# Where six subtractions run and in which order two loads are issued, in an attention and expert kernel on one core

## The chip, the cores and the metric

The kernel runs on one core of a Trainium2 chip. The metric is the device time of one execution in microseconds; the time before is the median of 3 runs, 727.25 us (727.22 to 727.77). The engines are named as in the profile: PE is TensorE's matmuls, PEld its weight loads, DVE is VectorE, ACT is ScalarE, POOL is GpSimd, and SP is the sync engine, whose list issues most of the DMAs. Each engine works through its own list of instructions in order.

## The reference, cut to what matters

```python
def _attn_ref(u, v, z):                       # u, v: 4 x 3072 x 256, z: 4 x 3072 x 64
    scores = (1.0 / S) * np.matmul(z, z.transpose(0, 2, 1))
    out = np.matmul(np.maximum(scores, 0.0) ** 2, v)
    return u * out
...
x = attn_out.reshape(B * S, D)
x = _moe_ref(x, w_gate, w1, w2, capacity)     # 8 experts, top 1, capacity slots each
return _moe2_ref(x, w_in, w_out)              # x * sigmoid-gated MLP
```

The gate sends each token to one of 8 experts, and an expert keeps only its first 384 tokens. Most rows beyond the first 3,500 tokens or so are dropped, so that the kernel works out attention for the first batch (3072 queries) and for one chunk of 384 queries of the second batch, and goes on only if some expert is not full by then.

## The kernel before, in words

All matrix products are done in a split form: a number is written as a head in fp32r and a low part, the rest in fp32r, and a product is the sum of two or three matmuls on heads and low parts. The splits are elementwise work for ACT, DVE and POOL.

**Attention.** The queries go in chunks: six of 512 queries (batch 0), then one of 384 queries (batch 1). A chunk takes KT = 24 steps, one per tile of 128 keys, so the stretch has 168 ticks. `attend` (L514) writes out the order by hand. In tick t it puts into the lists: `scores(t)` (L339: two matmuls, a relu on ACT L347, a square on DVE L352, or on ACT L350 in each fourth tick), `square(t-1)` (L355: the head ah by an ACT cast L360, the low part al by a DVE subtraction L361), `values(t-3)` (L364: six matmuls, the last two of which take al), and then whatever was booked for tick t with `at(t, f)`, in the order of booking (`Stream`, L250). "al(k)" below is the subtraction of step k; it stands in tick k+1, and TensorE takes it in tick k+3.

**Keys and values.** The keys of a batch are held in six tiles kz (groups g = 0 to 5 of four key tiles) and the values in six pairs of tiles big. For z, the raw tile zr (two buffers, shared with the raw queries zq of a chunk) is loaded by SP (`load_z`, L281). Rows 0 to 63 and 64 to 127 both hold the same z. `split_z` (L294) writes the head into all 128 partitions of kz (L161 on POOL) and then replaces partitions 64 to 127 by the low part (L297, 64x512, two operands in SBUF). For v, `load_v` (L286) loads one of two raw tiles rawt, and `split_v` (L299) makes the heads with two ACT casts (L163) and the low parts with two POOL subtractions (L303), each 128x512.

**The second batch.** While the last full chunk (ticks 120 to 143) still runs, the tiles kz and big are refilled for batch 1 group by group (L849 to L853). Group g is split in tick 127, 132, 135, 139, 143, 147 for g = 0 to 5, and its loads are booked four ticks earlier (for g = 1, five ticks). Its keys are needed from tick 144 + 4g on.

**What else stands in POOL's list there.** The result of a chunk is gated, transposed, given its expert and scattered to disp with four indirect DMAs that POOL issues (`route` L495, `scatter` L463); for the fifth chunk they stand in tick 131, just ahead of the split of group 1, and what they send is finished by DVE (slots L457 to L461, row numbers L446). The raw queries of the last chunk are split on POOL in tick 138 (L161, L337). The weights w_in and w_out arrive as 64-bit words and are converted in the ticks between (`Convert`, L172): ACT L202, L203, DVE L205, L208, L210, L213, an ACT cast, and POOL L217, L220, L222.

**After attention** come the experts (about 319 to 466 us) and the gated MLP (to the end), with TensorE as good as without gaps.

Of the kernel before, what the change touches and what calls it, by code (L numbers as in the profile page):

```python
# [28 lines left out]
def attention_moe_swish_kernel(  # L29
# [13 lines left out]
    nc = tc.nc  # L43
# [206 lines left out]
    class Stream:  # L250
# [5 lines left out]
        def at(self, t, f):  # L256
            self.todo.setdefault(t, []).append(f)
# [541 lines left out]
    def batch(b):  # L799
        return Batch(lambda r, n: v[b, r:r + n, :], lambda c, n: zT[:, b * S + c:b * S + c + n])  # L800


    b0, b1 = batch(0), batch(1)
# [4 lines left out]
    at = st.at  # L808
# [39 lines left out]
            at(c * KT - 6, lambda c=c: chunks[c].split(nc.gpsimd))  # L848
    for g in range(NG):  # L849
        t = TL - KT + (g + 1) * GK + LAG  # L850
        at(t - 4, lambda g=g: (b1.load_z(g), b1.load_v(g)))
        t += g == 1
        at(t, lambda g=g: (b1.split_z(g, nc.gpsimd, nc.gpsimd), b1.split_v(g, eng=nc.scalar)))  # L853

    free = [t for t in range(CV_A, TL + CV_B) if (t < KT or CV_OFF <= (t - LAG + 1) % KT < KT - 1)]
    cvs = list(conversions())
# [402 lines left out]
```

## Time and profile before

| | |
|---|---|
| median of 3 runs | 727.25 us (727.22 to 727.77) |
| the profiled execution's own time | 727.94 us |
| its span, from the first to the last instruction | 726.2 us |
| mean granted TensorE clock | 0.999 |
| busy: PE, PEld | 712.7 us, 634.3 us |
| busy: DVE, ACT, POOL | 521.0 us, 502.6 us, 264.7 us |

The span is 1.74 us shorter than the execution's own time, and the profiled execution is 0.69 us above the median. In the timeline each row is a start, a duration, the engine, the line of the kernel, the operation, its output and inputs, and in square brackets how long the engine sat idle just before and what ended that. A row with x2 merges two instructions that follow each other.

### The profile page before, as it was taken

Reading aid. Unit: us, or ns where it says so; the run is one execution under the profiler, and the core shown is the slowest. Engines: PE = TensorE matmul, PEld = TensorE weight load, DVE = VectorE, ACT = ScalarE, POOL = GpSimd, SP = SyncE. Lnnn points to the kernel's source line nnn. Section 1 sums busy time; section 2 is a strip of 40 time slices with the busy share of each in tenths; the row PEclk is TensorE's granted clock in tenths of the full one; section 3 lists DMA queues with packets and bytes.
Section 4 is the critical chain, followed back from the end, with each engine's and each line's share of the span. In section 5 each row is a group of like instructions: output and inputs, shape, how many; then the busy total and the mean of one; then the engine's idle time right before and its main releaser. Section 6 shows DMA issues by size and latency. Waiting matters only on the chain.

```text
span 726.2 us, 11358 instructions
## 1 busy us (share of the span) xinstructions
PE 712.7 (98%) x3954; PEld 634.3 (87%) x3955; DVE 521.0 (72%) x955; ACT 502.6 (69%) x986; POOL 264.7 (36%) x246
## 2 busy tenths in 40 slices
PE   9999999999999998999999999999999999999995
PEld 6888888888888887998999999999999999989895
DVE  6786877877778774863677777779767966676780
ACT  6777778777787896865676666667657755665771
POOL 8770505405243289455577676000004000040004
PEclk9999999999999999999999999999999999999999
DMA  5843515234056323363555554101001000010001
GB/s 181 288 146 123 183 35 188 70 116 146 10 199 212 98 93 98 112 190 107 192 195 178 172 177 140 58 27 54 1 1 59 1 1 1 1 58 1 1 1 59
DMA packets 50668, 72.18 MB, mean 99 GB/s; under 512 B 3446, under 2 KB 38684, under 8 KB 50608
## 3 DMA queue, kind: packets, MB, share of 16 engines
q1 hardware_dynamic: 48160, 65.03, 27.4%
q0 software_dynamic: 2448, 6.39, 2.4%
q8 instruction: 32, 0.52, 0.3%
q14 instruction: 28, 0.23, 0.1%
HBM read 46.05 MB, written 25.77 MB: 99 GB/s over the span
## 4 chain that ended last, share of the span: by engine, by line
PE 51%; issue 1%; POOL 0%; POOLq 0%; ACT 0%
PE ps_s L782 18%; PE ps_s L242 8%; PE ps_a L242 8%; PE ps_a L1071 6%; PE ps_a L1072 5%; PE ps_a L1073 5%; PE ps_a L600 1%; POOL out L793 0%; POOLq L1255 0%; ACT qt L606 0%; POOLq L793 0%
## 5 line engine op out<-in xcount | busy, mean ns | idle before, releaser
L242 PE MATMUL ps_a<-ah,big 128*128 128x512 f32 (+1 forms) x672 | 183.1, 389 | 2.7 <-ACT ah L360 2.5
L242 PEld LDWEIGHTS ps_a<-ah,big 128*128 128x128 f32 x672 | 123.9, 188 | 24.1 <-ACT ah L360 3.1
L361 DVE TENSOR_TENSOR al<-ps_s,ah 128x512 fp32r<-128x512 f32 (+1 forms) x168 | 111.3, 663 | 29.3 <-ACT ah L360 29.3
L347 ACT ACTIVATE r<-ps_s 128x512 f32<-128x512 f32 (+1 forms) x168 | 98.3, 585 | 42.0 <-PE ps_s L242 34.9
L352 DVE TENSOR_TENSOR ps_s<-ps_s,r 128x512 f32<-128x512 f32 (+1 forms) x132 | 89.2, 676 | 41.6 <-ACT r L347 40.1
L793 POOL DMA_INDIRECT out<-rows,ids x24 | 25.0, 1044 | 242.8 <-ACT rows L790 235.0
L782 PEld LDWEIGHTS ps_s<-wo,big 128*128 128x128 f32 x792 | 103.2, 190 | 6.1 <-ACT rows L790 1.1
L242 PE MATMUL ps_s<-qt,kz 128*128 128x512 f32 (+1 forms) x336 | 106.1, 392 | 0.5 <-POOL qt L337 0.5
L782 PE MATMUL ps_s<-wo,big 128*128 128x256 f32 x792 | 105.2, 282 | 0.8 <-ACT rows L790 0.8
L568 POOL TENSOR_TENSOR big<-rawt,big 128x512 fp32r<-128x512 f32 x64 | 89.7, 1429 | 42.4 <-ACT big L163 37.8
L242 PE MATMUL ps_a<-al,big 128*128 128x512 f32 (+1 forms) x336 | 101.1, 382 | 0.0
L360 ACT CAST ah<-ps_s 128x512 fp32r<-128x512 f32 (+1 forms) x168 | 95.6, 569 | 3.9 <-DVE ps_s L352 3.6
L242 PEld LDWEIGHTS ps_s<-qt,kz 128*128 128x128 f32 x336 | 63.6, 191 | 12.0 <-POOL qt L337 0.9
L242 PEld LDWEIGHTS ps_a<-al,big 128*128 128x128 f32 x336 | 62.6, 188 | 11.7 <-DVE al L361 0.4
L465 POOL DMA_INDIRECT disp<-xr,idx x27 | 28.5, 1054 | 107.3 <-ACT ps_s L350 79.8
L242 PE MATMUL ps_a<-qt,big 128*128 128x384 f32 x336 | 59.8, 335 | 0.2 <-ACT qt L606 0.2
L242 PEld LDWEIGHTS ps_a<-qt,big 128*128 128x128 f32 x336 | 58.3, 188 | 0.8 <-ACT qt L606 0.5
L163 ACT CAST big<-rawt 128x512 fp32r<-128x512 f32 x86 | 51.5, 621 | 6.2 <-DMA rawt<-in_v 5.4
L1094 DVE TENSOR_TENSOR big<-sg,big 128x512 fp32r<-128x512 f32 x66 | 45.1, 687 | 7.1 <-ACT big L1093 5.8
L1084 DVE TENSOR_TENSOR sg<-ps_a,sg 128x512 f32<-128x512 f32 x72 | 47.8, 684 | 1.8
L782 PEld LDWEIGHTS ps_s<-wo,late_c 128*128 128x128 f32 x348 | 45.9, 189 | 2.6
L1093 ACT CAST big<-sg 128x512 fp32r<-128x512 f32 x66 | 41.0, 622 | 10.2 <-DVE sg L1084 9.7
(227 smaller groups left out, 1243.8 us busy)
## 6 DMA issues: line engine op xcount, KB each, us to landing
rawt<-in_w SPq DMA_DIRECT2D x32, 512.0 KB, 5.2
out<-zero SPq DMA_DIRECT2D x16, 768.0 KB, 7.2
rawt<-in_v SPq DMA_DIRECT2D x11, 512.0 KB, 4.1
rawt<-in_w_in SPq DMA_DIRECT2D x8, 512.0 KB, 5.0
disp<-empty SPq DMA_DIRECT2D x6, 528.0 KB, 7.0
xg<-disp SPq DMA_DIRECT2D x8, 396.0 KB, 3.3
zr<-in_zT SPq DMA_DIRECT2D x12, 256.0 KB, 4.0
ut<-in_uT SPq DMA_DIRECT2D x6, 512.0 KB, 4.3
```

What stands on the lines that cost most here:

```text
L163: eng.copy(hi, x)
L242: nc.tensor.matmul(*a, **k)
L347: nc.scalar.activation(r[:, :Q], s[:, :Q], AF.Relu)
L352: nc.vector.tensor_mul(s[:, :Q], s[:, :Q], r[:, :Q])
L360: nc.scalar.copy(ah[:, :Q], a[:, :Q])
L361: nc.vector.tensor_sub(al[:, :Q], a[:, :Q], raw(ah[:, :Q]))
L568: nc.gpsimd.tensor_sub(ls[q][:, cs], rawt[r0 + q][:, cs], raw(hs[q][:, cs])))
L782: nc.tensor.matmul(o, lhsT=w[:, cs], rhs=wo[:, f, c:c + D], start=m not in self.seen, stop=last and n == 2, skip_group_check=True)
L1071: nc.tensor.matmul(ps, lhsT=ah, rhs=th, start=start, stop=False, skip_group_check=True)
L1084: nc.vector.tensor_mul(sg, src, sg)
L1093: nc.scalar.copy(gh, g)
L1094: nc.vector.tensor_sub(gl, g, raw(gh))
```

## The change

In the loop that books the refill for the second batch, two lines change. SP issues the load of v ahead of the load of z. The low part of the keys is made by DVE instead of POOL; the head stays on POOL, and all ticks stay.

```diff
     for g in range(NG):
         t = TL - KT + (g + 1) * GK + LAG
-        at(t - 4, lambda g=g: (b1.load_z(g), b1.load_v(g)))
+        at(t - 4, lambda g=g: (b1.load_v(g), b1.load_z(g)))
         t += g == 1
-        at(t, lambda g=g: (b1.split_z(g, nc.gpsimd, nc.gpsimd), b1.split_v(g, eng=nc.scalar)))
+        at(t, lambda g=g: (b1.split_z(g, nc.gpsimd, nc.vector), b1.split_v(g, eng=nc.scalar)))
```

In DVE's list the subtraction of group g stands in its tick behind al(t-1), and ahead of what DVE has in tick t+1: the square of step t+1 (L352) and al(t).

## Rows read from the trace of the kernel before

**Rows 1.** The page, part 1: busy time, share of the span, instructions

```profile
PE 712.7 (98%) x3954; PEld 634.3 (87%) x3955; DVE 521.0 (72%) x955; ACT 502.6 (69%) x986; POOL 264.7 (36%) x246
```

**Rows 2.** Waits from 230 to 320 us: total us, times, longest

```profile
PE ps_a L242 <- ACT ah L360: 2.5, 1, 2.5
...
PE ps_s L242 <- POOL qt L337: 0.5, 1, 0.5
```

**Rows 3.** Timeline of PE: where it takes al, and its longest wait

```profile
259.85 0.62 PE L242 MATMUL ps_a<-al,big 128*128 128x512 f32 x2
...
265.29 0.62 PE L242 MATMUL ps_a<-al,big 128*128 128x512 f32 x2
...
272.54 0.62 PE L242 MATMUL ps_a<-al,big 128*128 128x512 f32 x2
...
282.08 1.19 PE L242 MATMUL ps_a<-ah,big 128*128 128x512 f32 x4 [2.55 <-ACT ah L360]
```

**Rows 4.** Timeline of ACT: the heads of v, group 4

```profile
280.03 1.14 ACT L163 CAST big<-rawt 128x512 fp32r<-128x512 f32 x2 [4.58 <-DMA rawt<-in_v]
```

**Rows 5.** Timeline of SP's queue: the loads of group 4

```profile
275.62 0.34 SPq L283 DMA_DIRECT2D zr<-in_zT  x1
276.06 0.38 SPq L289 DMA_DIRECT2D rawt<-in_v  x1
```

**Rows 6.** Timeline of POOL, 246 to 276 us

```profile
246.80 2.54 POOL L303 TENSOR_TENSOR big<-rawt,big 128x512 fp32r<-128x512 f32 x2 [9.60 <-ACT big L163]
...
258.00 0.98 POOL L465 DMA_INDIRECT disp<-xr,idx  x1 [0.30 <-issue]
258.99 0.65 POOL L161 TENSOR_SCALAR kz<-zr 128x512 fp32r<-128x512 f32 x1
260.60 1.29 POOL L297 TENSOR_TENSOR kz<-zr,kz 64x512 fp32r<-64x512 f32 x1 [0.96 <-PE ps_a L242]
261.97 2.70 POOL L303 TENSOR_TENSOR big<-rawt,big 128x512 fp32r<-128x512 f32 x2
264.62 1.75 POOL L217 TENSOR_TENSOR c<-c,c 128x512 f32<-128x512 f32 x1
...
271.32 2.56 POOL L303 TENSOR_TENSOR big<-rawt,big 128x512 fp32r<-128x512 f32 x2
273.99 0.51 POOL L161 TENSOR_SCALAR qt<-zq 128x384 fp32r<-128x384 f32 x1
...
275.55 1.29 POOL L217 TENSOR_TENSOR c<-c,c 128x512 f32<-128x512 f32 x1
```

**Rows 7.** Timeline of DVE, 247 to 272 us

```profile
247.72 0.70 DVE L352 TENSOR_TENSOR ps_s<-ps_s,r 128x512 f32<-128x512 f32 x1 [0.84 <-ACT r L347]
...
255.61 0.68 DVE L361 TENSOR_TENSOR al<-ps_s,ah 128x512 fp32r<-128x512 f32 x1
...
257.62 0.68 DVE L361 TENSOR_TENSOR al<-ps_s,ah 128x512 fp32r<-128x512 f32 x1
...
261.23 0.69 DVE L361 TENSOR_TENSOR al<-ps_s,ah 128x512 fp32r<-128x512 f32 x1 [1.31 <-ACT ah L360]
261.84 0.42 DVE L208 TENSOR_SCALAR c<-c 128x512 int32<-128x512 int32 x1
...
263.38 0.68 DVE L361 TENSOR_TENSOR al<-ps_s,ah 128x512 fp32r<-128x512 f32 x1
263.98 1.24 DVE L210 SCALAR_TENSOR_TENSOR c<-rawt,c 128x512 int32<-128x512 int32 x1
...
266.33 0.41 DVE L213 TENSOR_SCALAR c<-c 128x512 int32<-128x512 int32 x1
...
268.52 0.69 DVE L361 TENSOR_TENSOR al<-ps_s,ah 128x512 fp32r<-128x512 f32 x1 [0.58 <-ACT ah L360]
```

**Rows 8.** Line 210 by itself: duration in ns, min/median/max, first and last start

```profile
L210 DVE SCALAR_TENSOR_TENSOR c<-rawt,c x13: 674/680/1239, 35.1 to 264.0; 128x512 int32<-128x512 int32 x13
```

**Rows 9.** Windows: busy of PE, PEld, DVE, ACT, POOL, then PEclk, DMA share, GB/s

```profile
279.00:282.00 3.00, 0.53 (x3) 0.19 (x1) 0.41 (x1) 1.97 (x5) 2.92 (x3) 1.00 0.39 118
```

## The prediction

> **What bounds the kernel now.** I read the page first: PE is busy 98% of the span and its weight loads 87% [rows 1], while VectorE has over a quarter of its time free on average. So work that leaves GpSimd or joins VectorE costs or gains only through TensorE's waits, and what TensorE loses at one place is not caught up later. Then the waits of the stretch where the second batch is refilled: TensorE stops just twice there, 0.51 us for the low part of the last chunk's queries on GpSimd, and 2.55 us for a head ah from ScalarE [rows 2, 3]. The second has its root in the loads. ScalarE stood 4.58 us in front of the cast of v's group 4, until its DMA landed at 280.03 [rows 4]; SP issued that load at 276.06, behind the load of z at 275.62, which had waited for a raw tile that GpSimd gave back [rows 5]. The tile that v needed was free when GpSimd ended its pair at 271.32 + 2.56 = 273.88 [rows 6]. GpSimd is the late engine: its list runs without a gap from 261.97 on [rows 6].
>
> So the two edits aim at 3.06 us of TensorE's time at most. What speaks against them is in VectorE's list: each moved subtraction stands between al(t-1) and the next square and al, which TensorE needs within few ticks, and it waits for a head that stands in GpSimd's late list.
>
> **The loads.** SP issues the same twelve DMAs, v ahead of z in each pair. Alone this brings the load of v's group 4 forward from 276.06 to 273.88, 2.2 of the 2.55 us [rows 3, 5, 6]. With the subtractions moved as well, both orders come out the same: GpSimd's pair ends earlier against TensorE, and z's buffer does too. Behind v, z is issued some 0.4 us later (the step from 275.62 to 276.06 [rows 5]); its head stands several us behind in GpSimd's list, which covers that. So: nothing of its own.
>
> **The subtraction.** GpSimd loses six of 1.29 us, and the 0.96 us that it sat idle ahead of the second [rows 6]. VectorE gains six of two SBUF operands by 512 columns. The nearest row is L210, also with two operands in SBUF: 0.68 us in the median, and 1.24 us once [rows 8]. That once is instructive: it began at 263.98 while GpSimd's pair ran to 261.97 + 2.70 = 264.67, and ended at 265.22, 0.55 us behind that [rows 6, 7]; and GpSimd's next instruction, begun at 264.62, took 1.75 instead of 1.29 us, as if it had begun anew at 265.1 [rows 6]. One waits for the other to end. So a subtraction costs 0.68 us, or, when GpSimd's own next instruction is first, 0.55 us behind the end of that. GpSimd's next is the pair of v, 2.54 / 2 = 1.27 us each [rows 6]; in its list it stands right behind the head and waits for nothing of VectorE. I take GpSimd as first.
>
> *Group 0.* VectorE gets there at 247.72 - 0.84 = 246.88 [rows 7]; the head is long done. GpSimd's pair has begun at 246.80 [rows 6], the subtraction ends at 246.80 + 1.27 + 0.55 = 248.62, 0.9 us behind the 247.72 at which VectorE's next began. al has 259.85 - (257.62 + 0.68) = 1.55 us in hand further on [rows 3, 7], so TensorE loses nothing; but the slots and row numbers that the scatters need come 0.9 us later, and the scatters with them.
>
> *Group 1.* The scatters end at 258.98 [rows 6], now about 259.9; the head behind them takes 0.65, to 260.5. VectorE has been at its place since 255.61 + 0.68 = 256.3, or 257.2 with the delay [rows 7]. First of the pair to 261.8, subtraction to 262.35. Behind it a square and al(132) of 0.7 and 0.68: 263.7. TensorE took al(132) at 259.85 [rows 3]. Lost: 3.8 us.
>
> *Group 2.* GpSimd: second of the pair to 263.6, three conversion steps (1.29 each [rows 6]) to 267.5, head to 268.1, first of the pair to 269.4; subtraction to 269.95. VectorE is there at 261.23 + 0.69 + 3.8 = 265.7 [rows 7]. Behind it L208 of 0.42, a square, al(135): 271.7. TensorE took al(135) at 265.29 [rows 3]. Lost so far: 6.4 us.
>
> *Group 3.* GpSimd: second of the pair to 271.2, the query split (275.55 - 273.99 = 1.56 [rows 6]) to 272.8. Then L217 waits for VectorE's L213, which began 2.95 us behind al(135) [rows 7]: 271.0 + 2.95 + 0.41 = 274.4. Two steps to 276.9, head to 277.5, first of the pair to 278.8, subtraction to 279.35. VectorE is there at 268.52 + 0.69 + 6.4 = 275.6 [rows 7]. Square and al(139): 280.7, against 272.54 [rows 3]. Lost: 8.2 us.
>
> *Groups 4 and 5.* By then VectorE is the later one; each costs it at most 1.27 + 0.55 us. I take nothing of TensorE's time; upper bound 1 us in all.
>
> *What goes away.* TensorE's last full step is 8 us later by then, so query split, load and cast of v are done in time: 3.06 us are given back [rows 2, 3].
>
> **Sum:** 8.2 - 3.06 = +5.1 us. The profiled execution stands 0.69 us above the median and 1.74 us above its span; a difference is carried to the median: 727.25 + 5.1 = **732.4 us**. Bounds of the unknown terms: if the 0.96 us wait that GpSimd had ahead of the second subtraction [rows 6] comes along to VectorE, +1; groups 4 and 5, +1; down, the cases below.
>
> The Trainium skill, page VectorE: DVE Perf Modes, section on two Vector instructions with no wait between them, says that an instruction whose operands begin at another quarter of the partitions starts only when all earlier ones have finished. The subtraction begins at partition 64 and its neighbours at 0. No row shows this case; here neighbours overlap by 0.68 - (263.98 - 263.38) = 0.08 us [rows 7], and by the rule the sum would be some 0.5 us higher (three subtractions on the path, two neighbours each).
>
> **The rivals.**
> *VectorE first.* If VectorE's request comes ahead of GpSimd's next instruction, the three subtractions end 0.68 us behind their heads: group 1 at 261.2, al(132) 262.6, lost 2.7; GpSimd, held up 0.68 each time, has head 2 at 268.2, al(135) 270.7, lost 5.4; head 3 at 276.6, al(139) 278.7, lost 6.1. Sum +3.0: 730.3. For it: the race at the end of a head is one of hundredths. Against: GpSimd's next starts without a wait, while VectorE must first see the head's end. On the SBUF — State Buffer page, section Who interferes with whom, the Trainium skill says that whichever of the two begins first keeps the shared port for its whole instruction; the 0.55 us of [rows 6, 7] agrees, and by the rule either this case or the first holds.
> *No waiting for each other.* Without group 0's delay: head 1 at 259.64, al(132) 261.7, lost 1.9; group 2 lost 3.8; group 3 lost 4.5. Sum +1.4: 728.7. Against it: L210.
> *Faster.* The whole 3.06 us come back and VectorE's waits fit in what al has in hand: 724.2. The point that decides is group 1: VectorE may be held for no more than 1.55 us beyond 256.3, so the head, 0.65 us, and the subtraction would have to be over by 257.9; the four scatters in front of the head end at 258.98 [rows 6]. It needs those to be ahead of their place before, and nothing in the change does that.
> *The clock.* The 2.55 us stop left the granted clock at 1.00 (2.4 GHz) [rows 9]; 3.8 us in one piece is longer than any stop seen here. If it falls to the level of 1.2 GHz, each 5 us at it cost 2.5: 735 or more.
> *Nothing moves,* because both effects cancel within 1.4 us, is the edge of the third case.
>
> **How the numbers follow.** GpSimd first 0.5 (731.4 to 734.4 with its bounds), VectorE first 0.22, no waiting 0.1 (half of it within the bound of same), clock 0.05, faster 0.08, no difference 0.05. A measurement of this kernel can tell about 0.2%, 1.45 us. That gives slower 0.82, same 0.1, faster 0.08. The range takes in the first three cases, 728.6 to 734.6, and leaves out 0.18. These are all but the faster one of one sign, so it needs no second range.
>
> **What would show it.** Right: idle time or long durations of VectorE (over 1.2 us) at the subtraction, most of all in group 1, just behind the scatters; TensorE waiting for al near 260, 267 and 274 us, together about 8 us; no more wait of ScalarE for v's group 4. If the subtractions of groups 1 to 3 last 0.7 us, VectorE was first. Wrong: no wait of TensorE at 260, which would mean that the head is done earlier than its place in GpSimd's list allows, or that VectorE's list is in another order than the code writes it. If the subtractions are cheap but TensorE still stops near 282 us, the loads did not do what I say.

## The result, and the profile after

The changed kernel takes **734.33 us** (median; 734.16 to 734.5) against 727.29 for the kernel before on the same chip (727.22 to 727.77): ratio 1.0096, 95% interval 1.0086 to 1.0107, +7.0 us. The forecast was 732.4, with 728.6 to 734.6 around it: the right sign, in the range, 2 us short. The profiled execution has a span of 732.6 and a mean granted clock of 0.992 (0.999 before).

Part 1 of the page after, busy time per engine:

```profile
PE 713.5 (97%) x3954; PEld 634.5 (87%) x3955; DVE 535.5 (73%) x961; ACT 502.7 (69%) x986; POOL 258.5 (35%) x240
```

Against [rows 1], GpSimd has six instructions and 6.2 us less, and VectorE six more and 14.5 us more: 2.4 us for each subtraction, where the line that was nearest to it takes 0.68 [rows 8]. TensorE is busy for 0.8 us more; the other 5.6 of the 6.4 us by which the span grows are idle time of TensorE.

The waits of the refilling, 230 to 325 us (total us, times, longest):

```profile
PE ps_a L242 <- DVE al L361: 9.1, 3, 7.5
...
DVE kz L297 <- POOL kz L161: 4.2, 2, 3.4
...
POOL qt L161 <- DMA zq<-in_zT: 1.4, 1, 1.4
```

Both waits of [rows 2] are gone. In their place TensorE waits for the low part al, and VectorE waits for GpSimd's heads. TensorE's timeline, the three places that [rows 3] name first, then the place of its old 2.55 us stop:

```profile
267.67 1.22 PE L242 MATMUL ps_a<-al,big 128*128 128x512 f32 x2 [7.48 <-DVE al L361]
...
275.40 0.73 PE L242 MATMUL ps_a<-al,big 128*128 128x512 f32 x2 [0.55 <-DVE al L361]
...
284.36 0.73 PE L242 MATMUL ps_a<-al,big 128*128 128x512 f32 x2 [1.06 <-DVE al L361]
...
290.58 1.09 PE L242 MATMUL ps_a<-ah,big 128*128 128x512 f32 x4
```

Taking the same matmuls of [rows 3] off these starts gives how late TensorE is at each place, in us:

| | al(132) | al(135) | al(139) | the old stop |
|---|---|---|---|---|
| forecast | 3.8 | 6.4 | 8.2 | 5.1 |
| measured | 7.82 | 10.11 | 11.82 | 8.50 |

Between the last two places the delay falls from 11.82 to 8.50: the two old stops, 3.06 us, are given back, and 0.26 more. On the way to the end the two profiled executions come closer still, to 6.4: by 0.8 in small steps and by most of the rest in the last 10 us, where the one before waits for ScalarE and this one does not. Nor do swap_only and keys129 below, whose subtractions stay on GpSimd, so I count that as the profiled execution's own; it stood 0.69 us above its median.

Why 7.8 in place of 3.8? VectorE's timeline:

```profile
247.06 1.68 DVE L297 TENSOR_TENSOR kz<-zr,kz 64x512 fp32r<-64x512 f32 x1
...
260.77 5.39 DVE L297 TENSOR_TENSOR kz<-zr,kz 64x512 fp32r<-64x512 f32 x1 [3.37 <-POOL kz L161]
266.19 0.70 DVE L352 TENSOR_TENSOR ps_s<-ps_s,r 128x512 f32<-128x512 f32 x1
...
271.04 1.68 DVE L297 TENSOR_TENSOR kz<-zr,kz 64x512 fp32r<-64x512 f32 x1
...
281.08 1.78 DVE L297 TENSOR_TENSOR kz<-zr,kz 64x512 fp32r<-64x512 f32 x1 [0.78 <-POOL kz L161]
```

and GpSimd's beside it:

```profile
246.90 2.99 POOL L303 TENSOR_TENSOR big<-rawt,big 128x512 fp32r<-128x512 f32 x2 [10.93 <-ACT big L163]
...
259.10 0.98 POOL L465 DMA_INDIRECT disp<-xr,idx  x1 [0.30 <-ACT r L347]
260.08 0.65 POOL L161 TENSOR_SCALAR kz<-zr 128x512 fp32r<-128x512 f32 x1
260.68 2.49 POOL L303 TENSOR_TENSOR big<-rawt,big 128x512 fp32r<-128x512 f32 x2
263.12 1.27 POOL L217 TENSOR_TENSOR c<-c,c 128x512 f32<-128x512 f32 x1
264.34 1.26 POOL L220 TENSOR_TENSOR c<-c,wo 128x512 f32<-128x512 f32 x1
265.68 1.61 POOL L222 TENSOR_TENSOR wo<-c,c 128x512 fp32r<-128x512 f32 x1
```

In groups 0, 2 and 3 the subtraction lasts about 1.7: GpSimd's first instruction of the pair, 1.27, and some 0.4 to 0.55 behind it. In group 1 it lasts 5.39. It starts at 260.77, just after GpSimd's pair at 260.68, and ends at 266.16, which is 0.56 behind 264.34 + 1.26 = 265.60, the end of the *fourth* GpSimd instruction. GpSimd runs those four with no time between them (each starts some 0.05 before the end printed for the one ahead); the first gap is the 0.08 ahead of 265.68. There GpSimd waits for itself, since L222 reads what L220 has just written; the same 0.08 stands ahead of L222 in tick131 below.

Then the clock. Windows after (busy us of PE, PEld, DVE, ACT, POOL with counts; PEclk; DMA share; GB/s):

```profile
258.00:262.00 4.00, 2.18 (x10) 1.49 (x8) 1.23 (x1) 1.07 (x3) 3.69 (x5) 1.00 0.28 101
262.00:266.00 4.00, 0.00 (x0) 0.00 (x0) 4.00 (x1) 0.00 (x0) 3.92 (x4) 0.75 0.30 102
266.00:270.00 4.00, 2.33 (x6) 1.85 (x7) 3.08 (x6) 3.05 (x6) 1.87 (x2) 0.50 0.31 96
270.00:274.00 4.00, 4.00 (x17) 3.26 (x16) 3.62 (x3) 2.79 (x6) 2.99 (x2) 0.90 0.05 10
```

TensorE stands still for 7.5 us; within the stop the granted clock goes from 1.00 to 0.50 (2.4 to 1.2 GHz), at 264.0, and it is back at 270.8. Only the 3 us or so after the restart cost anything beyond the stop: the matmuls behind the stop run at half rate, and TensorE falls back from 7.82 to 9.39 us.

### The profile page after: what moved, and what is told of

It reads as the page before. It is cut to its first block, busy times and chain, and to the rows that moved or that the text cites. A ratio compares the mean times of both kernels' runs of the same rounds, so it can differ in the third digit from the quotient of the medians.

```text
span 732.6 us, 11361 instructions
## 1 busy us (share of the span) xinstructions
PE 713.5 (97%) x3954; PEld 634.5 (87%) x3955; DVE 535.5 (73%) x961; ACT 502.7 (69%) x986; POOL 258.5 (35%) x240
## 4 chain that ended last, share of the span: by engine, by line
PE 51%; issue 0%; POOL 0%; POOLq 0%; ACT 0%
PE ps_s L782 18%; PE ps_s L242 8%; PE ps_a L242 8%; PE ps_a L1071 5%; PE ps_a L1072 5%; PE ps_a L1073 5%; PE ps_a L600 1%; POOL out L793 0%; POOLq L1255 0%; ACT qt L606 0%; POOLq L793 0%
## 5 line engine op out<-in xcount | busy, mean ns | idle before, releaser
L352 DVE TENSOR_TENSOR ps_s<-ps_s,r 128x512 f32<-128x512 f32 (+1 forms) x132 | 89.3, 677 | 31.4 <-ACT r L347 30.0
```

Source lines behind the costliest of these rows:

```text
L352: nc.vector.tensor_mul(s[:, :Q], s[:, :Q], r[:, :Q])
```

## The experiments

All times in us; each group of lines was timed against the kernel before on its own chip.

| run | time | before | ratio (95% interval) | longest L297 of 64x512 on VectorE | longest stop of TensorE, 240 to 300 |
|---|---|---|---|---|---|
| the change | 734.33 | 727.29 | 1.0096 (1.0086 to 1.0107) | 5.39 | 7.5 |
| low_only | 734.04 | 726.74 | 1.0102 (1.0085 to 1.0119) | 5.39 | 7.5 |
| swap_only | 726.18 | 726.74 | 0.9995 (0.9985 to 1.0004) | none | 1.3 |
| dummy | 728.77 | 726.74 | 1.0028 (1.0017 to 1.0040) | none | 0.9 |
| tick131 | 731.99 | 726.74 | 1.0074 (1.0057 to 1.0091) | 1.77 | 4.9 |
| stop | 732.08 | 726.99 | 1.0069 (1.0054 to 1.0085) | 1.77 | 3.8 |
| no_stop | 734.58 | 726.99 | 1.0104 (1.0088 to 1.0119) | 5.51 | 7.6 |
| group1_gpsimd | 734.11 | 726.99 | 1.0098 (1.0082 to 1.0113) | 1.78 | 9.0 |
| late_scatter | 734.59 | 727.40 | 1.0094 (1.0077 to 1.0111) | 2.96 | 8.1 |
| stop_ahead | 732.68 | 727.40 | 1.0079 (1.0057 to 1.0100) | 1.78 | 4.2 |
| early_queries | 724.97 | 726.99 | 0.9974 (0.9963 to 0.9984) | none | 1.4 |
| keys129 | 722.84 | 726.88 | 0.9948 (0.9934 to 0.9961) | none | none |

### Each half of the change alone: low_only and swap_only

```diff
# low_only: the loads as before
-        at(t - 4, lambda g=g: (b1.load_v(g), b1.load_z(g)))
+        at(t - 4, lambda g=g: (b1.load_z(g), b1.load_v(g)))
# swap_only: the low parts as before
-        at(t, lambda g=g: (b1.split_z(g, nc.gpsimd, nc.vector), b1.split_v(g, eng=nc.scalar)))
+        at(t, lambda g=g: (b1.split_z(g, nc.gpsimd, nc.gpsimd), b1.split_v(g, eng=nc.scalar)))
```

> Only the subtraction moves to VectorE; the loads keep their old order. If the held list of VectorE at group 1 makes the loss (theory A), the load order does not matter once TensorE is some 8 us late: 734.3 within 0.5, with the same subtraction of over 5 us near 260 us. If the order of the loads has a part in the loss or in what is given back (theory C), the time differs by 1 us or more from 734.3.

> Only the loads are swapped; the subtraction stays on GpSimd. Theory A: the load of v's group 4 goes from 276.06 to 273.9 us and lands 2.2 us earlier, TensorE's stop of 2.55 us near 282 us shrinks to some 0.4 us: 725.2. Rival: the time is given back, since the load of group 5 still waits for GpSimd, which is then the later one, and ScalarE stands in front of the cast of group 5 instead: 726.5 to 727.3.

The subtractions alone give the whole loss, with the same 5.39 us at the same place. With them, the order of the loads is worth nothing, as the prediction said.

The loads alone were expected to gain by theory A and gained nothing that the measurement can tell. The trace shows the gain and its loss. Timeline of TensorE in swap_only, its stops between 270 and 300 us:

```profile
275.63 0.44 PE L242 MATMUL ps_s<-qt,kz 128*128 128x384 f32 x1 [0.38 <-POOL qt L337]
...
280.06 1.20 PE L242 MATMUL ps_a<-ah,big 128*128 128x512 f32 x4 [0.54 <-ACT ah L360]
...
288.75 0.50 PE L392 MATMUL ps_a<-identw,ut 128*128 128x136 f32 x2 [1.33 <-ACT xr L398]
```

The stop of 2.55 shrinks to 0.54, which is the 2.0 us that an earlier load of v was to bring. Eight us later stands a new stop of 1.33. Timeline of ScalarE in swap_only, which stands in front of the cast of v's next group there:

```profile
278.00 1.14 ACT L163 CAST big<-rawt 128x512 fp32r<-128x512 f32 x2 [2.44 <-DMA rawt<-in_v]
...
286.52 1.14 ACT L163 CAST big<-rawt 128x512 fp32r<-128x512 f32 x2 [2.92 <-DMA rawt<-in_v]
```

ScalarE waited for group 4's v by 2.44 in place of 4.58 [rows 4], and then 2.92 for group 5's. Behind that wait stands xr, for which TensorE stops. Of the 2.0 us, 0.5 are left at 289 us and none at 303: the wait moved one group on.

### Are collisions of single instructions enough? dummy

The loads swapped, the low parts on GpSimd, and in each group's place in VectorE's list a subtraction of the same shape (raw keys minus themselves, into a tile that nothing reads) that waits for no head.

```diff
+ nc.vector.tensor_sub(warm[64:], b1.zr[g][64:], b1.zr[g][64:])
```

> Loads swapped, the real subtraction stays on GpSimd, and VectorE does at the same six places a subtraction of the same shape that waits for no head (raw keys minus themselves into a scrap tile, so it leaves nothing out of the result). Theory A (what costs is the wait for the head and what GpSimd has ready behind it): under 2 us above the run with the loads alone. Theory B (VectorE's time and its collisions with GpSimd as such, 6 x 1.7 us or more): 5 us or more above that run.

It costs 728.77 - 726.18 = 2.6 us over swap_only, so neither theory's figure came out: six more instructions with two SBUF operands on VectorE, beside a busy GpSimd, cost about a third of what the change lost. The six last 0.69 to 1.83, TensorE waits at most 0.9 at once, and the granted clock stays at 1.00 from 245 to 300 us. Group 1's ran at 257.19, while GpSimd still issued the scatters, so this run does not test what follows them.

### Which group holds TensorE up? tick131 and group1_gpsimd

```diff
# tick131: group 1 one tick earlier, ahead of the scatters
-        t += g == 1
# group1_gpsimd: group 1's low part stays on GpSimd
-        at(t, lambda g=g: (b1.split_z(g, nc.gpsimd, nc.vector), b1.split_v(g, eng=nc.scalar)))
+        at(t, lambda g=g: (b1.split_z(g, nc.gpsimd, nc.gpsimd if g == 1 else nc.vector), b1.split_v(g, eng=nc.scalar)))
```

> The changed kernel with group 1 split in tick 131, ahead of the four scatters in GpSimd's list, instead of tick 132 behind them. Theory A: the head of group 1 is done before VectorE gets there, so the stop of TensorE near 260 us goes (no subtraction over 2 us there). GpSimd is no earlier for group 2, and VectorE is not held up before it, so VectorE now waits at group 2 for its head, 4 us or more, and the loss comes back there in part: 729 to 734. If the loss came from the scatters alone, nothing takes its place: 725.

> The changed kernel with the subtraction of group 1 alone left on GpSimd. Theory A: nothing holds VectorE near 260 us, but it comes to group 2 some 4 to 7 us ahead of that head in GpSimd's list, TensorE stops there for 3 us or more, and the time is 730 to 735. Theory B (each subtraction costs its share of the loss): a sixth less than the changed kernel, 733.1. If group 1 alone is what is wrong with the change: 725 to 726.

In both, the long subtraction is gone and the stop moves on to group 2. In group1_gpsimd it is the longest of all, here in the waits of 240 to 300 us:

```profile
PE ps_a L242 <- DVE al L361: 9.0, 1, 9.0
...
DVE kz L297 <- POOL kz L161: 8.1, 2, 7.2
```

VectorE reaches group 2's subtraction early and waits 7.2 us for a head that stands in GpSimd's list behind group 1's pair and three conversion steps. So taking one group off VectorE does not help: a late head, with a subtraction of 1.74 behind it, is enough for a stop of 9.0. In tick131 TensorE has two stops, 1.3 for group 1 and 4.9 for group 2. Both times lie in the range that was expected.

### What keeps VectorE out of four instructions? stop and no_stop, late_scatter and stop_ahead

The first two runs put a small copy between the two instructions of group 1's pair. In stop it reads what the first has written, so that GpSimd waits for itself; in no_stop it reads a constant, and nothing waits.

```diff
 nc.gpsimd.tensor_sub(big[2 * g + 1][:, cs], rawt[g % NR][:, cs], raw(big[2 * g][:, cs]))
+if stop and c == c0:
+    nc.gpsimd.tensor_copy(scrap, raw(big[2 * g + 1][:, :1]))   # stop
+    nc.gpsimd.tensor_copy(scrap, ident[:, :1])                 # no_stop
```

> The changed kernel with one tiny GpSimd copy (128x1) between the two subtractions of v's group 1, that reads what the first has written and so makes GpSimd wait for its own end. Theory A1: the subtraction of 5.39 us near 260 us is that long because GpSimd's next four instructions start before the one in front has ended, so that the shared reads never come free; with a gap after the first, VectorE gets in there: about 1.8 us long, TensorE stops near 260 us for 3.8 to 4.2 us instead of 7.5, and the time is 730 to 732. Rival A2 (VectorE has to wait until GpSimd's list runs dry, or for the DMAs of the scatters): still 5 us or more, 734 or more.

> The control of the run before: the same tiny copy at the same place, but of a constant, so that GpSimd does not wait for its own end. Theory A1: no gap, VectorE's subtraction stays at 5 us or more (about 0.1 longer) and the time at 734.3 to 734.6. If any further instruction between the two lets VectorE in, it goes to 1.8 us as in the run before.

The line of the subtraction (L298 here, one line further down) by itself, in stop and then in no_stop (ns min/median/max, first and last start):

```profile
L298 DVE TENSOR_TENSOR kz<-zr,kz x9: 289/1678/1769, 3.9 to 292.2; 64x512 fp32r<-64x512 f32 x6, 64x128 fp32r<-64x128 f32 x2, 64x256 fp32r<-64x256 f32 x1
```

```profile
L298 DVE TENSOR_TENSOR kz<-zr,kz x9: 290/1682/5514, 3.8 to 294.8; 64x512 fp32r<-64x512 f32 x6, 64x128 fp32r<-64x128 f32 x2, 64x256 fp32r<-64x256 f32 x1
```

GpSimd's list in stop, the first of the pair and the copy:

```profile
260.88 1.27 POOL L304 TENSOR_TENSOR big<-rawt,big 128x512 fp32r<-128x512 f32 x1
262.22 0.55 POOL L306 COPY scrap<-big 128x1 f32<-128x1 f32 x1
```

and in no_stop:

```profile
260.64 1.28 POOL L304 TENSOR_TENSOR big<-rawt,big 128x512 fp32r<-128x512 f32 x1
261.85 0.20 POOL L306 COPY scrap<-ident 128x1 f32<-128x1 f32 x1
```

A gap of 0.07 us in GpSimd's list (260.88 + 1.27 = 262.15, then 262.22) lets VectorE in; one more instruction without a gap does not. The times are 732.08 and 734.58, 2.5 us apart; stop's lies just over the 730 to 732 that were given. The rest of the loss is there without the hold.

But GpSimd runs instructions one behind the other in other places too, and there VectorE gets in behind the first. Group 1 alone has the four scatters directly ahead of its head. late_scatter sets them three ticks later, so that group 2 has them instead; stop_ahead leaves them and makes GpSimd wait for itself once, between them and the head.

```diff
# late_scatter
-            st.at(t + 4 if last else t + 5, self.scatter)
+            st.at(t + 4 if last else t + 8 if self is chunks[nb0 - 2] else t + 5, self.scatter)
# stop_ahead
+        if g == 1:
+            at(t, lambda: (nc.gpsimd.tensor_copy(scrap[0], ident[:, :1]), nc.gpsimd.tensor_copy(scrap[1], scrap[0])))
```

> The changed kernel with the four scatters of the fifth chunk three ticks later: they stand behind group 1 and its three conversion steps in GpSimd's list and directly ahead of the head of group 2. Open is what keeps VectorE out of four GpSimd instructions in a row at group 1 (5.39) where it gets in behind the first everywhere else (1.68 to 1.78). Theory S (scatters directly ahead do it): group 1's subtraction takes 0.7 to 1.8 now, with the same pair and the same three conversion steps behind it, and the long one, over 1.8, is group 2's. Rival R (the place does it: a pair and three conversion steps without a wait between them): group 1's subtraction stays over 4. The time says little here, since VectorE must wait for group 2's head behind the scatters by either: 729 to 734.

> The changed kernel with two copies of one column on GpSimd between the scatters and the head of group 1; the second reads what the first writes, so GpSimd waits for itself once, ahead of the head, and not between the head and the pair of v. Theory S1 (after its scatters GpSimd's instructions follow each other more tightly until it has waited once): group 1's subtraction takes 1.7 to 1.8 and the time is that of the run with the wait behind the first of the pair, 731.5 to 732.8. Rival (only a wait at the boundary itself lets VectorE in): 5.3 to 5.6, and 734.3 to 735.2.

VectorE's subtractions of groups 1 and 2 in late_scatter:

```profile
257.43 1.57 DVE L297 TENSOR_TENSOR kz<-zr,kz 64x512 fp32r<-64x512 f32 x1
...
269.87 2.96 DVE L297 TENSOR_TENSOR kz<-zr,kz 64x512 fp32r<-64x512 f32 x1 [6.01 <-POOL kz L161]
```

GpSimd around them in the same run:

```profile
257.15 3.00 POOL L303 TENSOR_TENSOR big<-rawt,big 128x512 fp32r<-128x512 f32 x2 [6.70 <-ACT big L163]
260.11 1.30 POOL L217 TENSOR_TENSOR c<-c,c 128x512 f32<-128x512 f32 x1
...
268.20 0.97 POOL L465 DMA_INDIRECT disp<-xr,idx  x1 [0.30 <-issue]
269.19 0.64 POOL L161 TENSOR_SCALAR kz<-zr 128x512 fp32r<-128x512 f32 x1
269.78 2.48 POOL L303 TENSOR_TENSOR big<-rawt,big 128x512 fp32r<-128x512 f32 x2
```

Theory S holds on both sides. Group 1 has the same pair and the same conversion steps behind it as in the changed kernel, no scatters ahead, and takes 1.57. Group 2 has the scatters ahead and is held through both instructions of its pair, to 272.83, which is 0.57 behind 269.78 + 2.48 = 272.26; then GpSimd has nothing to do. The time, 734.59, lies just over the 729 to 734 that were given: the 6.01 us for the head came on top.

stop_ahead, VectorE at group 1:

```profile
261.23 1.75 DVE L298 TENSOR_TENSOR kz<-zr,kz 64x512 fp32r<-64x512 f32 x1 [3.73 <-POOL kz L162]
```

With one wait of GpSimd for itself ahead of the head the hold is gone, and the time, 732.68, is S1's. So it is the scatters' wake: VectorE does not get in between the elementwise instructions that follow GpSimd's indirect DMAs, until GpSimd has waited once. Two copies without a wait at this place were not run; but in no_stop an extra copy did not end the hold. tick131 fits as well. There the conversion steps stand between the scatters and group 2's head, with L222's wait among them (264.99 + 1.31 = 266.30, then 266.38), and GpSimd then runs the head and the pair without a wait:

```profile
262.75 0.98 POOL L465 DMA_INDIRECT disp<-xr,idx  x1 [0.30 <-issue]
263.73 1.33 POOL L217 TENSOR_TENSOR c<-c,c 128x512 f32<-128x512 f32 x1
264.99 1.31 POOL L220 TENSOR_TENSOR c<-c,wo 128x512 f32<-128x512 f32 x1
266.38 1.29 POOL L222 TENSOR_TENSOR wo<-c,c 128x512 fp32r<-128x512 f32 x1
267.64 0.62 POOL L161 TENSOR_SCALAR kz<-zr 128x512 fp32r<-128x512 f32 x1
268.24 2.92 POOL L303 TENSOR_TENSOR big<-rawt,big 128x512 fp32r<-128x512 f32 x2
```

VectorE's subtraction of group 2 takes 1.75 there. Why the wake is so inside the engine these runs don't show.

### A version that beats both: early_queries and keys129

In early_queries the low parts stay on GpSimd, the loads are swapped, and the last chunk's raw queries are loaded 14 and split 13 ticks earlier, in a stretch where GpSimd is idle. keys129 also splits group 1's keys three ticks earlier.

```diff
-            at(c * KT - (11 if c < nb0 else 8), chunks[c].load)
-            at(c * KT - 6, lambda c=c: chunks[c].split(nc.gpsimd))
+            at(c * KT - (11 if c < nb0 else 22), chunks[c].load)
+            at(c * KT - (6 if c < nb0 else 19), lambda c=c: chunks[c].split(nc.gpsimd))
...
# keys129, on top
-        at(t, lambda g=g: (b1.split_z(g, nc.gpsimd, nc.gpsimd), b1.split_v(g, eng=nc.scalar)))
+        at(t - 3 * (g == 1), lambda g=g: b1.split_z(g, nc.gpsimd, nc.gpsimd))
+        at(t, lambda g=g: b1.split_v(g, eng=nc.scalar))
```

> All subtractions on GpSimd as before, the loads swapped, and the load and the split of the last chunk's raw queries booked 14 and 13 ticks earlier, when GpSimd is idle. Theory A: GpSimd, late near 270 us, has 1.6 us less to do there; the stop of 0.5 us for the queries goes, the pair of group 3 ends earlier, so the load of group 5 does too and less of the gain of the swap is given back: 724 to 725.5. Rival: no gain against the run with the loads alone, 726.2, since group 5 waits for something else.

> The lows are on GpSimd, the load of v stands in front of that of the keys, the last chunk's queries are split earlier, and now also group 1's keys are split three ticks earlier, ahead of the scatters, in GpSimd's empty stretch of 249 to 254. Theory A (GpSimd's list from the scatters to group 3 sets when raw v is free, so when the loads of v start): GpSimd is rid of 0.65 (head) + 1.29 (low) + 0.96 (its wait) = 2.9 in the stretch after the scatters, the load of v for group 4 starts near 271.4 in place of 274.28, the 1.39 that TensorE still waits for the split of v goes, and the time is 723.3 to 724.2. Rival: the loads do not bind there (another wait takes the place, as it did when the loads alone were swapped), and the time stays at 724.6 to 725.3.

early_queries takes 724.97, and one stop of 1.39 us is left, for a head that stands behind ScalarE's wait for v. keys129 takes 722.84, a little under theory A's 723.3. GpSimd and SP in keys129:

```profile
249.20 0.62 POOL L161 TENSOR_SCALAR kz<-zr 128x512 fp32r<-128x512 f32 x1
249.91 1.30 POOL L297 TENSOR_TENSOR kz<-zr,kz 64x512 fp32r<-64x512 f32 x1
```

```profile
271.04 0.37 SPq L289 DMA_DIRECT2D rawt<-in_v  x1
```

The keys of group 1 now stand in the idle time ahead of the scatters, v's group 4 is loaded at 271.04 (276.06 before [rows 5]; 271.4 was forecast), and TensorE has no wait left between 240 and 300 us. Both versions have the new load order as well, which brought nothing alone; no run has the shorter list with the old order, so what each of the two gives is not shown.

## Why the prediction was right, and what was too small

**The outcome and the main reason held.** The path is the one forecast: scatters, head, subtraction, al, TensorE. Without the hold, TensorE's stop for al(132) is the one forecast: 3.81 in stop, where 3.8 was forecast. That the whole loss in stop, 732.08 - 726.99 = 5.09, meets the forecast +5.1 as well is luck: its parts behind group 1 are others. The low clock took about 2.9 us that the sum did not have, groups 2 and 3 took 2.0 in place of 4.4, and 3.45 instead of 3.06 were given back.

**The step that failed is group 1's** "First of the pair to 261.8, subtraction to 262.35": the term of 3.8 measured 7.65 (7.82 less the 0.15 to 0.2 that TensorE was late already). The prediction let VectorE in behind the *first* GpSimd instruction, by the one case in the trace, L210, which got in behind the instruction that was running [rows 6, 7]. It got in behind the fourth: 3.81 us later than forecast (266.16 against 262.35), which is what the three further instructions take (265.60 - 261.8 = 3.80). The row of L210 was read rightly, but it stands at a place where GpSimd had waited since its scatters: the 0.96 us ahead of its own subtraction [rows 6]. The change took that subtraction, and so that wait, out of GpSimd's list.

**The clock** had a chance of 0.05 as a case of its own. It fell, and that in each run above with a stop of 3.8 or more. The price per time was right (half of what is worked at 1.2 GHz), but the case was not a rival to the others: it comes on top of a long stop. It took 1.57 us in the changed kernel, and the 735 or more that were given for it were not reached.

**Groups 2 and 3** were too large: 2.6 and 1.8 were forecast, and the steps from 9.39 to 10.11 and on to 11.82 are 0.7 and 1.7, of which the waits in brackets are 0.55 and 1.06. While VectorE was held, GpSimd went on; head 2 was done at 267.25 + 0.61 = 267.86 as forecast (268.1), but VectorE came at 271.04 in place of 265.7 and waited for no head. One late engine had overtaken the other. The errors partly cancel: +3.85 for the hold, +1.57 for the clock, -2.0 for groups 2 and 3, -0.3 in what was given back, +0.2 that TensorE was late already, and -2.1 on the way from there to the end. With the forecast +5.1 that gives 6.3 of the 6.4 us between the two profiled executions; the medians are 7.0 apart, since the one before stood 0.69 above its median. That the time lies inside the range, 0.3 us below its upper end, is therefore luck: with the hold alone the forecast would have been 727.25 + 5.1 + 3.85 = 736.2.

**Group 0** was right: the subtraction ends at 247.06 + 1.68 = 248.74 (248.62 forecast). TensorE lost at most 0.2 there, and the scatters ended at 260.08, some 1.1 late (0.9 forecast). **Groups 4 and 5** cost TensorE nothing. **What goes away** was right: no wait for the queries and none for v's group 4 is left. **The loads** were right beside the subtractions (low_only), and wrong in the clause on the loads alone: 2.0 of the forecast 2.2 us appeared, and a wait one group later took them back.

**The rivals.** "VectorE first" and "no waiting for each other" fall by groups 1 and 3, where the two engines set off from the same head: the subtraction takes 5.39 and 1.78, against 0.69 for one alone in dummy. GpSimd was first in each group here; in groups 0 and 2 its pair had begun 0.16 us before VectorE came.

The Trainium skill's page VectorE: DVE Perf Modes, section on two Vector instructions with no wait between them, is borne out: the instructions around the subtraction start 0.03 behind the end of the one ahead (260.77 + 5.39 = 266.16, then 266.19), and not 0.08 before it. At some 0.1 for each, that is small beside the rest. The Trainium skill's page SBUF — State Buffer, section Who interferes with whom, says that the one that begins first has the shared port for its whole instruction; the 1.7 us rows agree, and the 5.39, held through four instructions, goes beyond it.

## What to carry to other kernels

Before elementwise work is moved to an engine with free time, look at what stands behind it in that engine's list and at how late its input is in the *other* engine's list: here a subtraction of under a microsecond put al behind GpSimd's scatters. A collision read at one place in a trace holds for that place; ask what runs ahead and behind at the new one, above all indirect DMAs of GpSimd, and give GpSimd a wait (or its work another place) where VectorE must get in. Work of the late engine moved into that engine's own idle time, with the loads swapped, brought 4 us, where moving it to another engine cost 7.

## What the runs showed of the hardware

- Behind GpSimd's four indirect DMAs, VectorE's subtraction with two operands in SBUF was held through four GpSimd instructions (5.39 us in the changed kernel; 5.51 in no_stop, with a fifth, short one among them), and through both of a pair (2.96) when the scatters stood ahead of another group (late_scatter). One wait of GpSimd for itself, ahead of the head (stop_ahead) or between the pair (stop), brings it back to 1.75. Without scatters directly ahead it takes 1.57 to 1.78 beside GpSimd's pair.
- The granted clock fell to the 1.2 GHz level after stops of 3.8, 4.2, 4.9, 7.5, 8.1 and 9.0 us, and not at 2.55 [rows 9]. It was low from 264.0 to 270.8 us in the changed kernel and from 263.3 to 270.1 in stop. With the 7.5 us stop over half of that lay in the stop itself; with the 3.8 us stop most of it lay behind, where TensorE worked: the same matmuls, taken against the kernel before, fell back from 7.8 to 9.4 us in the one and from 4.4 to 7.3 in the other. So a stop that was 3.8 us longer (no_stop against stop) cost only 2.5 us more in time (734.58 against 732.08).
